# Batch 0's last stage in a new order of row tiles, and its FFN1 in two token passes

## The chip, the cores and the metric

The kernel runs on one core of a Trainium2 chip. The metric is device time in microseconds (us): the median of several executions. Profiles show one execution, in microseconds from the start of its span. TensorE is PE in them (PEld are its weight loads), VectorE is DVE, ScalarE is ACT, GpSimd is POOL, and SyncE is SP.

## The reference

Eight batches of 448 tokens. An attention of 12 heads of 64 channels without softmax is followed by a Fourier mix over tokens and channels, a layer norm, and a two-layer network, each added to the stream:

```
scores = q @ k.T / sqrt(64);  attn = max(scores, 0)**2 / 448;  x = attn @ v      # (8, 448, 768)
mixed = real(fft(fft(x, axis=tokens), axis=channels));  u = x + mixed
un = (u - mean(u)) / sqrt(var(u) + 1e-6)                                          # over the 768 channels
out = u + max(un @ w_ch1, 0) @ w_ch2                                              # 768 -> 3072 -> 768
```

## The kernel before

The Fourier mix of the tokens is symmetric: the kernel computes 225 of the 448 rows (0 to 224) as a "top" and gets the others as a "bottom" in reversed order. It therefore keeps u in two DRAM tiles per batch, `utop` (tokens 0 to 223) and `ubot` (tokens 224 on), and writes the bottom with an indirect DMA on POOL whose row indices run backwards (`back`). The add at the end (`reload`, `add`) reads u again from both.

The order of all instructions is fixed when the program is built. Each part is a generator that yields what its next step needs (`need(engine, duration, ...)`), and a small planner (`Streams.run`) always takes the step that can start earliest by its own cost estimates. Each engine then executes its list in order. Waits between engines are semaphores that the tile framework adds from what each instruction reads and writes. That holds for DRAM tiles too: two writes of one tile are ordered.

PSUM has three double-bank tiles (`BS`, `psS`) and two single banks (`BF`, `psF`). Attention's scores (L537), squares (L558, L564) and values (L522) of batch b+1 run among the FFN matmuls of batch b. FFN1 (L1073) computes the hidden rows for a group of tokens, 24 blocks of 128 rows with six matmuls each; a relu (L1044 on DVE, L1046 on ACT) writes each block to `hT`; FFN2 (L1091) then runs over tiles of 128 tokens. The groups alternate between 384 and 512 tokens, so that two batches make seven tiles: group 0 holds tokens 0 to 383 of batch 0, and group 1 the last 64 of batch 0 and all of batch 1.

Batch 0 has nothing to overlap with and has a stage of its own, `first_tail`. It takes four row tiles: `t` = 0 and 2 are the top (128 and 112 rows), 1 and 3 the bottom (128 and 112 rows), some of them computed twice. For each of them

- `rows` (L605, L609) makes u in PSUM, in two halves of 384 channels,
- `stats`, `aggregate`, `root` and `scale` give mean and 1/std,
- `copy` (L658) brings u to SBUF for the store, and `norm` gives `un`: on POOL from the SBUF copy for tiles 0, 1 and 2 (L682), on ACT and DVE from PSUM for tile 3 (L684, L687),
- `turn` (L708) transposes `un` on PE, and `unload` (L723) copies it to `unT`, the moving operand of FFN1. Two turns are preceded by filler matmuls (L706) and one is followed by 16 of them (L713). A fifth turn (L775) brings the last 64 tokens into group 1.

`first_stores` issues the four stores of u: tiles 0 and 2 on SP (L876), tiles 1 and 3 on POOL (L879). The loads that POOL issues in the same stretch come from `load_group` (L300, q, k and v) and from `load_w2` (L339, four pieces of 1152 KB of the second weight matrix; here w2_0 to w2_3). FFN1 of group 0 starts when all four tiles are in `unT`.

Of the kernel before, what the change touches and what calls it, by code (L numbers as in the profile page):

```python
# [117 lines left out]
def mm(n):  # L118
    return n / 2400 + 0.006
# [18 lines left out]
def kernel(  # L138
# [54 lines left out]
    back = [const.tile([128, 1], mybir.dt.int32, name=f"back{i}") for i in range(2)]  # L193
    warm = const.tile([128, 512], BF16, name="warm")
# [386 lines left out]
    def first_tail(pcs):  # L581


        pus, helds, done, sts = [None] * 4, [None] * 4, [[None, None] for _ in range(4)], [None] * 4
        mvs, stds, rss, nms, uts, pts = ([None] * 4 for _ in range(6))
        t_st, t_mv, t_std, t_rn = ([0.0] * 4 for _ in range(4))
        t_un, t_u = [[0.0, 0.0] for _ in range(4)], [[0.0, 0.0] for _ in range(4)]

        def rows(t):
            ch, i = divmod(t, 2)  # L590
            s0, s1 = SC[ch]
            n = s1 - s0
            d = 4 * mm(D // 2) + 3 * 0.06
            e = yield need("PE", 2 * d, [pcs[0][1], pcs[1][1]] + x_ready[0], [BF, BF] if t == 3 else [BS])
            if t == 3:
                pu = helds[t] = [BF.take() for _ in range(2)]
            else:
                helds[t] = [BS.take()]
                pu = [helds[t][0][:, 0], helds[t][0][:, 1]]
            for hf in range(2):  # L600

                for w in range(2):
                    for a, (n0, n1) in enumerate(TC):
                        mat = seq[:n1 - n0, w, a, s0:s1] if w == 0 or i ^ hf else nseq[:n1 - n0, a, s0:s1]
                        nc.tensor.matmul(pu[hf][:n, 0:D // 2], lhsT=mat,  # L605
                                         rhs=pcs[a][0][:n1 - n0, w, hf:hf + D // 2],
                                         start=(w == 0 and a == 0), stop=False)
                for a in range(3):
                    nc.tensor.matmul(pu[hf][:n, a * 128:(a + 1) * 128],  # L609
                                     lhsT=xTc[5 - a if hf else a][:, i * XH + s0:i * XH + s1],  # L610
                                     rhs=rev if hf else ident, start=False, stop=(a == 2))
                done[t][hf] = e - (1 - hf) * d + LATENCY["PE"]
            pus[t] = [p[:n] for p in pu]
            if t == 3:
# [5 lines left out]
        def half(t, hf):  # L620

            return pus[t][hf][:, D // 2 - 1::-1] if hf else pus[t][hf][:, 0:D // 2]

        def stats(t, hf):
            n = SC[t // 2][1] - SC[t // 2][0]
# [3 lines left out]
            nc.vector.bn_stats(sts[t][:n, hf, :], pus[t][hf][:, 0:D // 2])  # L629

        def aggregate(t):
            n = SC[t // 2][1] - SC[t // 2][0]
            t_mv[t] = yield need("DVE", 0.2)
            mvs[t] = work.tile([128, 2, 2], FP32, name="mv", tag="mv", bufs=4)[:n]
            nc.vector.bn_aggr(mvs[t][:, 0, :], sts[t][:n])

        def root(t):
            n = SC[t // 2][1] - SC[t // 2][0]
            t_std[t] = yield need("ACT", 0.25, [t_mv[t] + LATENCY["DVE"]])
            stds[t] = work.tile([128, 2], FP32, name="std", tag="std", bufs=4)[:n]  # L640
            nc.scalar.activation(stds[t][:, 0:1], mvs[t][:, 0, 1:2], AF.Sqrt, bias=eps_t[:n])

        def scale(t):
            n = SC[t // 2][1] - SC[t // 2][0]
            e = yield need("DVE", 0.3, [t_std[t] + LATENCY["ACT"]])
            t_rn[t] = e + LATENCY["DVE"]
            rss[t] = work.tile([128, 2], FP32, name="rstd", tag="rstd", bufs=4)[:n, 0:1]
            nms[t] = work.tile([128, 2], FP32, name="nmr", tag="nmr", bufs=4)[:n, 0:1]
# [3 lines left out]
        def copy(t, hf, en):  # L652
            ch, i = divmod(t, 2)
            n = SC[ch][1] - SC[ch][0]
            e = yield need(en, (act if en == "ACT" else dve)(D // 2), [done[t][hf]], [BU[i]] if hf == 0 else [])
            if hf == 0:
                uts[t] = work.tile([128, D], FP32, name="u", tag=f"u{i}" if i else "u", bufs=2)
            (nc.scalar.copy if en == "ACT" else nc.vector.tensor_copy)(  # L658
                uts[t][:n, hf * (D // 2):(hf + 1) * (D // 2)], half(t, hf))
            t_u[t][hf] = e  # L660
            if t == 3:
                BF.give(helds[t][hf], e)
            if hf == 1:
                if t != 3:
                    BS.give(helds[t][0], max(t_u[t]))
                e = max(t_u[t])
                first_us[ch][i] = uts[t], e + LATENCY["ACT"], e
                u_done[ch][i].t = e + LATENCY["ACT"]

        def norm(t, hf, en):  # L670
            ch, i = divmod(t, 2)
            n = SC[ch][1] - SC[ch][0]
            deps = [t_rn[t]]
            if en == "POOL":
                deps.append(u_done[ch][i])
            d = {"ACT": act(D // 2), "DVE": dve(D // 2), "POOL": 2.0}[en]
            e = yield need(en, d, deps, [BUN[ch]] if i == 0 and hf == 0 else [])
            if uns[0][t] is None:
                uns[0][t] = work.tile([128, D], BF16, name="un", tag=f"un{t}", bufs=1)
            un = uns[0][t][:n]  # L680
            if en == "POOL":
                nc.gpsimd.tensor_scalar(un, uts[t][:n], rss[t], nms[t], op0=ALU.mult, op1=ALU.add)  # L682
            elif en == "ACT":
                nc.scalar.activation(un[:, hf * (D // 2):(hf + 1) * (D // 2)], half(t, hf), AF.Identity,  # L684
                                     bias=nms[t], scale=rss[t])
            else:
                nc.vector.tensor_scalar(un[:, hf * (D // 2):(hf + 1) * (D // 2)], half(t, hf), rss[t], nms[t],  # L687
                                        op0=ALU.mult, op1=ALU.add)
            t_un[t][hf] = e + LATENCY[en]
            if min(t_un[t]) or en == "POOL":  # L690
                half_un[ch][i].t = max(t_un[t])

        def turned_cols(t):

            return ((128, ident, 0, 128), (128, rev[:, 0:63], HS + 97, 63),
                    (96, ident[:96, :96], 128, 96), (97, rev[:97, 31:128], HS, 97))[t]

        def turn(t, k):
            n, idn, c0, w = turned_cols(t)
            un = uns[0][t]  # L700
            e = yield need("PE", 6 * 0.06 + 0.11 * k, [max(t_un[t])], [BS])
            pts[t] = [BS.take()]
            bank = [pts[t][0][:, 0], pts[t][0][:, 1]]
            for i in range(k):

                nc.tensor.matmul(bank[0][:, 0:256], lhsT=warm[:, 0:128], rhs=warm[:, 0:256], start=True, stop=True)  # L706
            for m in range(MC):
                nc.tensor.matmul(bank[m // 3][:, m % 3 * 128:m % 3 * 128 + w], lhsT=un[:n, m * 128:(m + 1) * 128],  # L708
                                 rhs=idn, start=True, stop=True)
            done[t] = [e + LATENCY["PE"]] * 2  # L710
            for i in range(16 if t == 1 else 0):

                nc.tensor.matmul(bank[0][:, 384:512], lhsT=warm[:, 0:128], rhs=warm[:, 0:128], start=True, stop=True)  # L713
            if t == 1:
                yield need("PE", 16 * 0.055)

        def unload(t, en):
            n, idn, c0, w = turned_cols(t)
            g = groups[0][2]
            src = pts[t][0][:, :, 0:384].rearrange("p h (m w) -> p h m w", w=128)[:, :, :, 0:w]  # L720
            dst = g[:, :, c0:c0 + w].rearrange("p (h m) w -> p h m w", h=2)
            last = yield need(en, (act if en == "ACT" else dve)(6 * w), [done[t][0]])
            (nc.scalar.copy if en == "ACT" else nc.vector.tensor_copy)(dst, src)  # L723
            BS.give(pts[t][0], last)
            first_un[t].t = last + LATENCY["ACT"]
# [437 lines left out]
```

## Time and profile before

| | |
|---|---|
| median of 3 runs (lowest to highest) | 609.27 us (608.72 to 610.45) |
| profiled execution: span, first to last instruction | 607.4 us |
| the same execution's time outside the span | not shown; median less span is 1.9 us |
| PE busy in the span | 595.4 us (98%) |
| first row matmul of `first_tail` (L605) | starts at 41.06 us |
| first FFN1 matmul of group 0 (L1073) | starts at 53.74 us |
| first FFN2 matmul of group 0 (L1091) | starts at 89.80 us |
| PE idle from 41.06 to 89.80 us | 0.91 + 0.35 + 0.51 us |

The span is that of one execution, and its steps are read from the trace; the median comes from other executions of the same program. A line of a timeline gives the start, the length, the engine, the source line, the operation with what it writes and reads, how often it comes, and the idle time before it with what ended that. The length of a run of matmuls includes the pipeline of the last one, so the spacing of matmuls is taken from start to start.

### The profile page before, as it was taken

What the parts mean: (1) busy time and instruction counts of PE and PEld (TensorE: products, weight loads), DVE (VectorE), ACT (ScalarE), POOL (GpSimd) and SP (SyncE); (2) the same over time, 40 slices, a digit from 0 to 9 for tenths busy, and PEclk for the clock granted to TensorE, in tenths of its full rate; (3) what the DMA queues carried; (4) which work ended last, traced back from release to release, by engine and by line L of the source; (5) the groups of instructions that cost most, each with busy time, mean ns of one, the idle gap of its engine ahead of it and who ended that gap; (6) DMA issues with size and microseconds to landing.
All of it is one profiled execution on the core that took longest, in us unless ns stands there. A gap on an engine that the chain in (4) does not pass through costs nothing.

```text
span 607.4 us, 10224 instructions
## 1 busy us (share of the span) xinstructions
PE 595.4 (98%) x4035; PEld 329.5 (54%) x4054; DVE 339.4 (56%) x766; ACT 293.3 (48%) x445; POOL 155.2 (26%) x200
## 2 busy tenths in 40 slices
PE   8999999989999999999999999999999999999997
PEld 7566556534555565555445565555445566654464
DVE  6977785876596568455834369645843447110011
ACT  5967661677544357436653167435761345014300
POOL 8433203311163137111710117210620006100000
PEclk9999999999999999999999999999999999999999
DMA  9999997888659967977593796985451215420022
GB/s 127 207 209 228 216 194 132 186 128 120 111 148 212 157 121 215 141 135 120 172 154 96 127 127 173 160 164 97 145 136 60 87 51 165 121 91 20 1 79 79
DMA packets 125216, 82.22 MB, mean 135 GB/s; under 512 B 76272, under 2 KB 113168, under 8 KB 125168
## 3 DMA queue, kind: packets, MB, share of 16 engines
q0 software_dynamic: 40320, 34.07, 34.4%
q1 hardware_dynamic: 84848, 47.50, 33.6%
q8 instruction: 32, 0.52, 0.4%
q14 instruction: 16, 0.13, 0.1%
HBM read 62.91 MB, written 26.69 MB: 148 GB/s over the span
## 4 chain that ended last, share of the span: by engine, by line
PE 83%; DVE 11%; ACT 4%; issue 1%; DVEq 0%; ACTq 0%
PE psF L1091 33%; PE psF L1073 32%; PE psF L522 6%; PE psS L537 6%; DVE sq L564 2%; PE psS L961 2%; ACT sq L558 2%; DVE stats L837 2%; PE psS L1113 1%; PE psS L805 1%; DVE u L826 1%; DVE u L825 1%; PE psS L605 1%; PE psF L421 1%; DVE tm L816 1%
## 5 line engine op out<-in xcount | busy, mean ns | idle before, releaser
L1073 PE MATMUL psF<-unT,w 128*128 128x384 bf16 (+1 forms) x1134 | 227.2, 352 | 1.4 <-issue 0.2
L558 ACT ACTIVATE sq<-psS 112x896 bf16<-112x896 f32 x192 | 164.8, 916 | 130.5 <-PE psS L537 130.4
L1091 PE MATMUL psF<-w,hT 128*128 128x384 bf16 (+2 forms) x1343 | 225.0, 326 | 0.8 <-DVE xT L448 0.7
L1091 PEld LDWEIGHTS <-hT 128*128 128x128 bf16 x1344 | 129.2, 98 | 93.4 <-issue 8.8
L1073 PEld LDWEIGHTS <-w 128*128 128x128 bf16 x1152 | 109.6, 98 | 109.3 <-issue 12.3
L1046 ACT ACTIVATE hT<-psF 128x512 bf16<-128x512 f32 (+1 forms) x180 | 98.6, 548 | 110.2 <-PE psF L1073 109.6
L564 DVE TENSOR_TENSOR sq<-sq 112x896 bf16<-112x896 bf16 x192 | 117.8, 635 | 44.6 <-ACT sq L558 43.3
L1054 DVE TENSOR_TENSOR o<-psF,o 128x384 f32<-128x384 f32 (+2 forms) x56 | 31.0, 553 | 106.2 <-PE psF L1091 105.9
L300 POOL DMA_DIRECT2D vn<-in_v_dram x24 | 17.3, 719 | 177.4 <-PE psF L522 156.9
L445 DVE TENSOR_SCALAR xT<-psF 128x224 bf16<-128x224 f32 x48 | 18.7, 389 | 71.7 <-PE psF L522 71.7
L537 PE MATMUL psS<-qkT 64*112 64x448 bf16 x384 | 52.3, 366 | 2.0 <-DVE unT L780 0.8
L522 PE MATMUL psF<-sq,vn 112*64 112x448 bf16 x384 | 45.9, 359 | 1.7 <-DVE sq L564 1.2
L825 POOL TENSOR_TENSOR u<-tp,xn 128x385 f32<-128x385 f32 (+1 forms) x14 | 15.5, 1108 | 117.0 <-DVE tp L816 94.7
L537 PEld LDWEIGHTS <-qkT 64*112 64x112 bf16 x384 | 20.8, 125 | 27.6 <-issue 21.6
L522 PEld LDWEIGHTS <-vn 112*64 112x64 bf16 x384 | 17.9, 109 | 24.2 <-issue 16.0
L854 POOL TENSOR_SCALAR un<-u,rstd,nmr 128x768 bf16<-128x768 f32 (+1 forms) x24 | 26.9, 1124 | 6.4 <-DVE nmr L846 6.0
L837 DVE BATCH_NORM_STATS2 stats<-u 128x6 f32<-128x384 f32 (+1 forms) x56 | 28.2, 539 | 0.0
L879 POOL DMA_INDIRECT ubot<-u,back x16 | 17.1, 1072 | 23.7 <-DVE hT L1044 19.3
L300 POOL DMA_DIRECT2D qn<-in_q_dram x21 | 15.3, 726 | 19.7 <-DVE qkr L389 10.8
L1113 PE MATMUL psS<-warm 128*128 128x126 bf16 (+1 forms) x204 | 17.9, 242 | 1.3 <-DVE warm L215 1.3
L448 DVE TENSOR_SCALAR xT<-psF 128x224 bf16<-128x224 f32 x48 | 18.4, 384 | 0.0
L456 DVE TENSOR_TENSOR fold<-xT 128x225 bf16<-128x225 bf16 x48 | 15.9, 331 | 2.1
(117 smaller groups left out, 369.1 us busy)
## 6 DMA issues: line engine op xcount, KB each, us to landing
out_dram<-o SPq DMA_DIRECT2D x27, 384.0 KB, 2.7
vn<-in_v_dram POOLq DMA_DIRECT2D x24, 224.0 KB, 5.0
qn<-in_q_dram POOLq DMA_DIRECT2D x21, 224.0 KB, 6.3
kn<-in_k_dram POOLq DMA_DIRECT2D x21, 224.0 KB, 7.2
w<-in_moe_w_ch_dram POOLq DMA_DIRECT2D x12, 384.0 KB, 14.1
w<-in_moe_w_ch_dram POOLq DMA_DIRECT2D x4, 1152.0 KB, 22.7
utop<-u SPq DMA_DIRECT2D x8, 384.0 KB, 2.6
o<-utop SPq DMA_DIRECT2D x8, 384.0 KB, 4.5
```

What stands on the lines that cost most here:

```text
L300: nc.gpsimd.dma_start(out=t, in_=src[b, hs].rearrange("h (p j) d -> p h (j d)", j=4))
L522: nc.tensor.matmul(av[h * Dh:(h + 1) * Dh, 0:S], lhsT=vn[:, c, h0 + h, :], rhs=sq[:, h, :], start=(c == 0), stop=(c == 3))
L537: nc.tensor.matmul(sc[:R, h, 0:S].rearrange("k (c q) -> k c q", c=4), lhsT=kT[ps, m % 2, c, :], rhs=qT[ps, m % 2], start=True, stop=True)
L558: nc.scalar.activation(r, sc[:R, :, 0:S], AF.Relu)
L564: nc.vector.tensor_tensor(r, r, r, op=ALU.mult)
L837: nc.vector.bn_stats(stats[:n, hf, :], u[:n, hf * (D // 2):(hf + 1) * (D // 2)])
L854: nc.gpsimd.tensor_scalar(un[:n], u[:n], rstd[:n, i:i + 1], nmr[:n, i:i + 1], op0=ALU.mult, op1=ALU.add)
L1046: nc.scalar.activation(h[:, 0:N], ph[:, 0:N], AF.Relu)
L1054: nc.vector.tensor_tensor(o[:, hs], pc[:, 0:w], o[:, hs], op=ALU.add)
L1073: nc.tensor.matmul(ph[:, 0:N], lhsT=w1_sb[m][hf][:, jj * 128:(jj + 1) * 128], rhs=unT[:, m, 0:N], start=(m == 0), stop=(m == MC - 1))
L1091: nc.tensor.matmul(pc[:, 0:w], lhsT=hT[j][:, c * 128:(c + 1) * 128], rhs=w2_sb[j // 6][:, j % 6, hs], start=(j == 0), stop=(j == JC - 1))
L1113: nc.tensor.matmul(first_pps[0][:, t, c0:512], lhsT=warm[:, 0:128], rhs=warm[:, c0:512], start=not begun, stop=False)
```

## The change

The four row tiles of batch 0 become 128, 128, 96 and 96 tokens and hold each token once: tile 0 is the top's rows 0 to 127, tile 1 the bottom's 128 rows that mirror 1 to 128, tiles 2 and 3 the rest. Group 0 now takes its tokens in this order (its third tile holds tile 2 and the first 32 columns of tile 3), group 1 the last 64 columns of tile 3 and batch 1. Reloads and output stores follow the token order in pieces.

`first_tail` runs `rows` of tiles 0, 1 and 2 one after the other, then tiles 0 and 1 to the end: their norms on ACT and DVE from PSUM, their turns into the two `psF` banks, their unloads split over ACT and DVE. Tile 3's `rows` stand among these steps. The rest of tiles 2 and 3 (`copies`, `later`) becomes streams of their own, which the planner places among the FFN's work: their norms run on POOL from the SBUF copies. The filler matmuls and the fifth turn are gone. Each tile's store is placed by itself (`store`).

FFN1 of group 0 runs in two passes over the 24 blocks: one on columns 0 to 255 (tiles 0 and 1), two blocks in a `psF` bank, and one on columns 256 to 383, four blocks in a bank; the second waits for all four tiles. The first needs tiles 0 and 1 alone. `hT` becomes six tiles of four blocks. Other groups run as before.

In the built program POOL's order from the w2 loads on was: w2_0, v, w2_1, w2_2, norm of tile 0, norm of tile 1, norm of tile 2, store of tile 1, w2_3, store of tile 3, loads of q, k and v. It is now: w2_0, v, w2_1, w2_2, w2_3, store of tile 1, norm of tile 2, store of tile 3, norm of tile 3, loads of q, k and v. On PE the six matmuls of tile 2's turn stand behind 18 of FFN1's first-pass matmuls, those of tile 3's turn behind 36.

```diff
+    first_back = [const.tile([128, 1], mybir.dt.int32, name=f"fback{i}") for i in range(2)]
...
+        for i, x in enumerate(first_back):
+            nc.gpsimd.iota(x, pattern=[[0, 1]], base=HS - 1 - 128 * i, channel_multiplier=-1)
...
+        widths = (128, 128, R - 16, R - 16)
...
+        def copy(t, hf):
+            i = t % 2
+            e = yield need("ACT", act(D // 2), [done[t][hf]], [BU[i]] if hf == 0 else [])
...
+            nc.scalar.copy(uts[t][:widths[t], hf * (D // 2):(hf + 1) * (D // 2)], half(t, hf))
+            t_u[t][hf] = e
+            if hf == 1:
+                copied[t].t = e + LATENCY["ACT"]
+                sch.add(store(t), (1, 1))
...
+        def store(t):
+            ch, i = divmod(t, 2)
+            n = widths[t]
+            if i:
+                e = yield need("POOL", 1.1, [copied[t]])
+                nc.gpsimd.indirect_dma_start(
+                    out=ubot[0], out_offset=bass.IndirectOffsetOnAxis(ap=first_back[ch][:n], axis=0),
+                    in_=uts[t][:n], in_offset=None)
+            else:
+                e = yield need("SP", 0.1, [copied[t]])
+                nc.sync.dma_start(out=utop[0][ch * 128:ch * 128 + n], in_=uts[t][:n])
+            u_stored[0][t].t = sch.dma(e, n * D * 4) + i
...
+        def norm(t, hf):
...
+            if hf is None:
+                e = yield need("POOL", 1.1, [t_rn[t], copied[t]])
+                nc.gpsimd.tensor_scalar(uns[t], uts[t][:widths[t]], rss[t], nms[t], op0=ALU.mult, op1=ALU.add)
+                t_un[t] = [e + LATENCY["POOL"]] * 2
+                used[t].t = e
+                return
+            en = ("ACT", "DVE")[hf]
...
+        def turn(t):
+            n = widths[t]
+            e = yield need("PE", 6 * 0.06, [max(t_un[t])], [BF, BF] if t < 2 else [BS])
...
+        def unload(t, hf):
+            n = widths[t]
+            en, cp = (("ACT", nc.scalar.copy), ("DVE", nc.vector.tensor_copy))[hf]
+            e = yield need(en, (act, dve)[hf](3 * n), [t_turn[t]])
...
+            for g, c0, w0, w1 in ((0, t * 128, 0, n),) if t < 3 else ((0, 352, 0, 32), (1, 0, 32, 96)):
+                cp(groups[g][2][:, 3 * hf:3 * hf + 3, c0:c0 + w1 - w0], src[:, :, w0:w1])
...
+        def later(t):
+            for hf in range(2):
+                yield from stats(t, hf)
+            yield from aggregate(t)
+            yield from root(t)
+            yield from scale(t)
+            yield need("SP", 0.0, [copied[t]])
+            free(t)
+            yield from norm(t, None)
+            yield from turn(t)
+            e = yield from unload(t, 0)
+            yield from unload(t, 1)
...
         for t in range(3):
-            yield from rows(t)
-            if t == 2:
-                yield from rows(3)
-            yield from stats(t, 0)
...
-        yield from copy(3, 1, "DVE")
+            for hf in range(2):
+                yield from rows(t, hf)
+        for step, t, *hf in ((stats, 0, 0), (copy, 0, 0), (stats, 0, 1), (aggregate, 0), (copy, 0, 1), (root, 0),
+                             (stats, 1, 0), (copy, 1, 0), (scale, 0), (norm, 0, 0), (stats, 1, 1), (aggregate, 1),
+                             (norm, 0, 1), (root, 1)):
+            yield from step(t, *hf)
+        free(0)
+        for step, t, *hf in ((turn, 0), (scale, 1), (norm, 1, 0), (norm, 1, 1), (rows, 3, 0), (unload, 0, 1), (unload, 0, 0),
+                             (turn, 1), (rows, 3, 1), (unload, 1, 0), (unload, 1, 1), (copy, 1, 1)):
+            yield from step(t, *hf)
+        free(1)
         tail[0] = 2
-        sch.add(turn_rows(uns[0][1], max(t_un[1]), 128, rev[:, 63:127], 0, 64, "DVE", second_un[0]), (1, 1))
+        for t in (2, 3):
+            sch.add(copies(t), (0.05 * t, 0.05 * t))
+            sch.add(later(t), (0.05 * t, 0.05 * t))
...
-            for t0, n in ((0, 384), (384, 512)):
+            for segs, n in (([(0, 128), (HS + 96, 128), (128, 128)], 384), ([(256, 64), (S, S)], 512)):
...
+        def first(k, c0, w):
+
+            for j0 in range(0, JC, k):
+                hf = j0 // (JC // 2)
+                for i in range(k):
+                    j = j0 + i
+                    q = j // 4
+                    e = yield need("PE", 6 * mm(w), [w1_ready[hf]] + (first_un if c0 else []),
+                                   ([] if i else [BF]) + ([BH[q]] if hT[q] is None else []))
...
+                    for m in range(MC):
+                        nc.tensor.matmul(ph[:, i * w:(i + 1) * w], lhsT=w1_sb[m][hf][:, jj * 128:(jj + 1) * 128],
+                                         rhs=unT[:, m, c0:c0 + w], start=(m == 0), stop=(m == MC - 1))
...
+                sch.add(relu(ph, e, j0, k, c0, w), (0, 0))
+            return e
+
+        if b == 0:
+            yield from first(2, 0, 256)
+            e = yield from first(4, 256, 128)
+        else:
+            e = yield from first(1, 0, N)
```

More of the change, by code (lines that the diff above doesn't have):

```diff
@@ L581, in first_tail @@
     def first_tail(pcs):
[L584 to L589, printed above, removed]
-            ch, i = divmod(t, 2)
[L591 to L614, printed above, removed]
@@ new lines, in half, with rows @@
+        def half(t, hf):
+            return pus[t][hf][:, D // 2 - 1::-1] if hf else pus[t][hf][:, 0:D // 2]
+        def rows(t, hf):
+            i, n = t % 2, widths[t]
+            e = yield need("PE", 4 * mm(D // 2) + 3 * 0.06, [pcs[0][1], pcs[1][1]] + x_ready[0], [] if hf else [BS])
+            if hf == 0:
+                held[t] = BS.take()
+                pus[t] = [held[t][:n, h] for h in range(2)]
+            pu = pus[t][hf]
+            for w in range(2):
+                for a, (n0, n1) in enumerate(TC):
+                    mat = seq[:n1 - n0, w, a, span(t, 0)] if w == 0 or i ^ hf else nseq[:n1 - n0, a, span(t, 0)]
+                    nc.tensor.matmul(pu[:, 0:D // 2], lhsT=mat, rhs=pcs[a][0][:n1 - n0, w, hf:hf + D // 2],
+                                     start=(w == 0 and a == 0), stop=False)
+            for a in range(3):
+                nc.tensor.matmul(pu[:, a * 128:(a + 1) * 128], lhsT=xTc[5 - a if hf else a][:, span(t, i * XH)],
+                                 rhs=rev if hf else ident, start=False, stop=(a == 2))
+            done[t][hf] = e + LATENCY["PE"]
+            if t == 3 and hf == 1:
@@ L670, in norm @@
[L670 to L715, printed above, removed]
@@ new lines, in free @@
+        def free(t):
+            BS.give(held[t], max([t_st[t]] + t_u[t] + ([x - 0.15 for x in t_un[t]] if t < 2 else [])))
+        def turn(t):
+            n = widths[t]
+            e = yield need("PE", 6 * 0.06, [max(t_un[t])], [BF, BF] if t < 2 else [BS])
+            pts[t] = [BF.take(), BF.take()] if t < 2 else [BS.take()]
+            bank = pts[t] if t < 2 else [pts[t][0][:, h] for h in range(2)]
+            for m in range(MC):
+                nc.tensor.matmul(bank[m // 3][:, m % 3 * 128:m % 3 * 128 + n], lhsT=uns[t][:, m * 128:(m + 1) * 128],
+                                 rhs=rev[:n, 128 - n:] if t % 2 else ident[:n, :n], start=True, stop=True)
+            pts[t].append(bank)
+            t_turn[t] = e + LATENCY["PE"]
@@ L1001, in mixes @@
             yield from mix(b)
[L1004 removed]
+    BH = [Bufs(1) for _ in range(JC // 4)]
     BO = Bufs(2)
@@ L1013, in ffn, with pieces @@
     def ffn(b):
-        T0, N, unT = groups[b]
+        segs, N, unT = groups[b]
         NC = N // 128
+        tokens = [t for t0, n in segs for t in range(t0, t0 + n)]
+        def pieces(c, bounds=False):
+            out, r = [], 0
+            while r < 128:
+                t, w = tokens[c * 128 + r], 1
+                while r + w < 128 and tokens[c * 128 + r + w] == t + w and not (bounds and (t + w) % HS == 0):
+                    w += 1
+                out.append((r, t, w))
+                r += w
+            return out
         work_us = JC * MC * mm(N) + NC * 2 * JC * mm(D // 2)
         os, ot = [None] * NC, [Cell() for _ in range(NC)]
-        hT, ht = [None] * JC, [Cell() for _ in range(JC)]
+        hT, ht = [None] * (JC // 4), [Cell() for _ in range(JC)]
         def advance(us):
```

183 lines of the change are left out of this document (74 added, 109 removed).

## The prediction

> **What bounds the kernel now.** I read the page first, then TensorE's timeline over batch 0's tail, then GpSimd's timeline and waits, then the landing times of single DMAs.
>
> ```profile
> PE 595.4 (98%) x4035; PEld 329.5 (54%) x4054; DVE 339.4 (56%) x766; ACT 293.3 (48%) x445; POOL 155.2 (26%) x200
> DMA  9999997888659967977593796985451215420022
> ```
>
> TensorE (PE) is busy 98% of the span and executes in order, so a change is worth the PE work it removes plus the PE idle it removes, less what it adds of either. The second line says the DMA engines are full over the first 15% of the span, where this change lies (0 to 91 us).
>
> TensorE's timeline at the end of the tail and at the first FFN2 matmul (columns: start, us, engine, line, op, count, idle before):
>
> ```profile
> 50.27 0.42 PE L708 MATMUL psS<-ident,un 96*128 96x96 bf16 x6
> 51.60 0.44 PE L708 MATMUL psS<-rev,un 97*128 97x97 bf16 x6 [0.91 <-ACT un L684]
> ...
> 52.90 0.40 PE L537 MATMUL psS<-qkT 64*112 64x448 bf16 x2 [0.35 <-DVE unT L723]
> ...
> 53.74 1.15 PE L1073 MATMUL psF<-unT,w 128*128 128x384 bf16 x6
> ...
> 65.73 0.95 PE L522 MATMUL psF<-sq,vn 112*64 112x448 bf16 x8 [0.51 <-ACT hT L1046]
> ...
> 89.80 2.11 PE L1091 MATMUL psF<-w,hT 128*128 128x384 bf16 x12
> ```
>
> From the first row matmul (41.06) to FFN2 (89.80) PE idles only 0.91+0.35+0.51 = 1.77 us. That, some filler matmuls and one turn are all there is to win.
>
> GpSimd's (POOL) timeline, then its longest waits on the stores:
>
> ```profile
> 49.16 0.98 POOL L682 TENSOR_SCALAR un<-u,rstd,nmr 112x768 bf16<-112x768 f32 x1 [0.64 <-DVE nmr L650]
> 50.31 1.11 POOL L879 DMA_INDIRECT ubot<-u,back  x1 [0.17 <-issue]
> 51.44 0.88 POOL L339 DMA_DIRECT2D w<-in_moe_w_ch_dram  x1
> 71.62 1.01 POOL L879 DMA_INDIRECT ubot<-u,back  x1 [19.30 <-DVE hT L1044]
> 72.62 0.75 POOL L300 DMA_DIRECT2D qn<-in_q_dram  x1
> ```
> ```profile
> POOL ubot L879 <- DVE hT L1044: 19.3, 1, 19.3
> ```
>
> This is the row that decides. The second indirect store into ubot0 stands 19.3 us. The releaser named is an unrelated relu; what ends the wait is the landing of the first store, which writes the same DRAM tile. First the landing of the store issued at 50.31, then of the w2 pieces issued at 43.49, 44.62 and 51.44:
>
> ```profile
> DMA to landing us min/median/max: 20.4/20.4/20.4
> ```
> ```profile
> DMA to landing us min/median/max: 20.2/20.2/20.2
> ```
> ```profile
> DMA to landing us min/median/max: 25.1/25.1/25.1
> ```
> ```profile
> DMA to landing us min/median/max: 26.9/26.9/26.9
> ```
>
> So w2_1 lands at 63.7, w2_2 at 69.7, the store at 70.7, w2_3 at 78.3: POOL's transfers land in the order of issue, each 1152 KB piece taking 5.5 to 7.6 us. And POOL is held as a whole: the load behind the second store started at 72.62, right after it. Before, nothing that PE needs soon stood behind that store; all three norms on POOL were ahead of it.
>
> **The change, part by part.**
>
> *Removed on PE.* Filler 5+3 matmuls of 256 columns (0.55+0.33 us at a spacing of 0.11) and 16 of 128 (0.89 at 0.0555), and the fifth turn (64 columns, 0.27): 2.04 us. With the 1.77 of idle, 3.81 us at best.
>
> *FFN1 of group 0.* 144 matmuls of 384 columns at 4.00/24 = 0.167 us (24.0) become 144 of 256 at 0.110 (L706's spacing) and 144 of 128 at 0.0555 (L713's spacing): 23.8. Zero. The merged relus are fewer (18 for 24) and beside PE.
>
> *The tail's new order.* Two engines' reads of one PSUM tile are kept in order, as ScalarE's timeline of before shows:
>
> ```profile
> 44.37 0.48 ACT L658 COPY u<-psS 128x384 f32<-128x384 f32 x1 [1.30 <-DVE stats L629]
> ```
>
> The copy only reads what the stats read, and waits for them. So stats and copies of a half alternate between VectorE (0.56) and ScalarE (0.48), about 0.1 per hand-over. Walking this with those durations: norm of tile 0 half 0 on ScalarE (0.68) ends at 46.9, half 1 on VectorE at 47.8; tile 1's at 48.9 and 49.6; its unloads end near 51.1. PE waits about 0.5, 0.7, 0.5 and 0.7 around the two turns, starts FFN1 at 52.1, then waits some 2.1 for ScalarE, whose first relu stands behind the four copies of tiles 2 and 3, and 0.6 around the next unload: 5.1 of new idle for 1.77 taken out. PE reaches the turn of tile 3 at about 60.4.
>
> *Tile 3's norm moves to POOL, behind the stores.* In the built program's order POOL has: w2_2, w2_3, store of tile 1, norm of tile 2, store of tile 3, norm of tile 3. The store of tile 3 waits for the landing of the store of tile 1 (both write ubot0), and norm 3 is queued behind it. PE's six turn matmuls of tile 3 wait for norm 3, and they stand inside FFN1's first pass, ahead of 108 of its 144 matmuls: all of PE waits. Also, w2_3 is now issued ahead of the store of tile 1 (at 45.5, when the q load issued at 39.13 has landed 6.4 us later), so the store lands behind one more 1152 KB piece. Landing: w2_1 at 63.7 as before; w2_2 and w2_3 at 5.5 each (w2_1's time; the transposes L477 that slowed them before, from 63.2, now wait for PE) 74.7; the store 1.0 later, as before: 75.7. With w2_3 at its old 7.6 and w2_2 at 69.7 it is 78.3, and 75.0 if the pieces take 5.15. Then 0.9 to the next issue (70.7 to 71.62 before), 1.0 for it, 0.1, and 0.98 for the norm (L682), 0.2 to PE: the turn starts at 78.9. PE stands still from 60.4 to 78.9, 18.5 us. Nothing covers this; ScalarE and VectorE run out of work too.
>
> *After the turn.* What remains on PE up to FFN2, counted in the built order and priced by spacings of the timeline and the chain: the turn (0.35), 108 FFN1 matmuls of 256 (11.9) and 144 of 128 (8.0), five groups of value matmuls L522 at 0.88 (4.4), six groups of score matmuls L537 at 0.71 and a pair at 0.33 (4.6), 32 transposes L421 (1.0): 30.25. The relus and squares beside it had 18 us to catch up, so I add no wait.
>
> *A cold array.* At the run's start PE's matmuls came 0.105 us apart until about 7.1, and the same 126 columns 0.055 afterwards, though the clock column says 1.00 there:
>
> ```profile
> 1.27 5.44 PE L1113 MATMUL psS<-warm 128*128 128x512 bf16 x44 [1.27 <-DVE warm L215]
> 9.93 0.72 PE L1113 MATMUL psS<-warm 128*128 128x126 bf16 x10
> ```
>
> If 18.5 us of standing still brings that state back, 5.8 us at half speed lose 2.9; if not, 0. No idle this long is in the trace; I take 2.9, the nearest row, and keep both ends. The Trainium skill, "TensorE: Matmul & The Clock Gate", Part 1, says that an idle window of about 3.4 us halves the clock and a busy one of 3.4 restores it; by that the loss is 1.7 (an estimate) and the sum 1.2 lower.
>
> *The rest at nothing.* Two more iotas on POOL fall into its 8.8 us of idle before 39.13. Reloads and output stores change in pieces, not bytes; the first reload from ubot0 needs store 3, landed by about 82, and its add comes after 109. POOL's next loads start at 79 instead of 72.6, but their readers on PE are 22 us later. If these covers failed, the loads would cost up to the 7 us by which they are late; PE's own delay rules it out.
>
> *Sum.* 78.9 + 30.25 + 2.9 = 112.05 for FFN2's start, against 89.80: +22.25. After it the work and the waits (2.2 us around 122 to 126) are the same. The span is 607.4 and the median of the runs 609.27; I leave the 1.9 us around the span as they are: **631.5**.
>
> **The rivals.**
>
> *A. The store of tile 1 lands early.* If it took the 7.3 us of the second store before, it would land at 58.2 and norm 3 be ready for PE at 61.4, hardly after its 60.4. Then the time is -3.8 + 5.1 + 1.0 (61.4 against 60.4) = +2.3: 611.6; landing before 57 it is +1.3: 610.6. Against it: 20.4 us for just this store. The Trainium skill, "DMA: Bandwidth & Descriptors", Anatomy of one DMA, gives about 2 us plus the bytes at 436 GB/s, under 3 us here (an estimate); the 20.4 measured decides against it. Chance 0.04.
>
> *B. Faster.* As A, and the tail's hand-overs cost less than I walked: PE's new idle falls below 3.8. With 2 us of it, 607.5; 605.5 with none. It decides at the turn of tile 3: norm 3 must be done by about 58. For it: filler and waits do go. Against it: POOL's 19.3 us row. Chance 0.04.
>
> *C. The narrow pass is bound by weight loads.* LDWEIGHTS takes 98 ns a piece (L1073), longer than a 128-column matmul's 55. If loads did not overlap, 144 x 0.0425 = 6.1 us more, on top of the hold: 637.6. Against it: L713, 16 matmuls each with its 98 ns load, 0.0555 apart. The Trainium skill, "TensorE: Matmul & The Clock Gate", Back-to-back issue gap, gives about 81 ns sustained at 128 columns: +3.7, 635.2 (an estimate). Chance 0.06.
>
> **How the numbers follow.** The hold as summed has 0.86, C 0.06, A 0.04 (its two prices stand on either side of 0.3%, so half of it counts as no change), B 0.04. The low end takes a warm array (-2.9), the landing at 75.0 (-0.7) and a microsecond of the later waits gone: 627. The high end takes the landing at 78.3 (+2.6) and two waits after the standstill that I did not walk, of the size of those near 122 and 125 (0.83 and 1.04): 636. A measurement of this kernel can tell about 0.3% (1.8 us) from no change: faster 0.04 (B), same 0.02, slower 0.94.
>
> **What would show it.** In the profile after: PE idle of about 18 us before six matmuls psS<-rev,un 96x96, near 60 to 79, put down to POOL un; POOL's second DMA_INDIRECT near 76.6 with 20 us or more of idle before it; the first one landing some 25 us after its issue near 51; matmuls after the wait about twice as far apart for some microseconds; first FFN2 matmul at about 112. The prediction is wrong if the first store lands before 60, if norm 3 starts ahead of the second store, or if PE's turn of tile 3 shows no long idle.

## The result, and the profile after

The changed kernel takes 629.91 us in the median (629.49 to 631.12), against 609.27 for the kernel before beside it: the ratio is 1.034 (95% interval 1.032 to 1.036), slower by 3.4%. The prediction was 631.5 with a range of 627 to 636. The profiled execution took 629.49 us with a span of 627.7.

From the page of the kernel after, the busy times, TensorE's row and the row of its granted clock:

```profile
PE 596.0 (95%) x4149; PEld 336.6 (54%) x4168; DVE 336.8 (54%) x765; ACT 295.0 (47%) x447; POOL 155.3 (25%) x201
PE   8996099999999999999999999999999999999997
PEclk9999589999999999999999999999999999999999
```

TensorE is as busy as before (596.0 us for 595.4) in a span that is 20.3 us longer. One slice of 15.7 us is empty, and the granted clock is down in the same slice and the next.

TensorE's timeline of the kernel after (start, us, engine, line, op, count, idle before), at the places shown of before:

```profile
54.96 0.39 PE L424 MATMUL psF<-ident,qn 112*64 112x112 bf16 x8 [1.63 <-ACT hT L1044]
...
57.87 1.48 PE L1082 MATMUL psF<-unT,w 128*128 128x256 bf16 x12
78.66 0.66 PE L710 MATMUL psS<-rev,un 96*128 96x96 bf16 x6 [19.31 <-POOL un L687]
79.12 4.03 PE L1082 MATMUL psF<-unT,w 128*128 128x256 bf16 x24
...
91.74 2.79 PE L1082 MATMUL psF<-unT,w 128*128 128x256 bf16 x24
94.47 0.78 PE L540 MATMUL psS<-qkT 64*112 64x448 bf16 x6
...
99.56 2.85 PE L1082 MATMUL psF<-unT,w 128*128 128x128 bf16 x48
102.36 0.95 PE L525 MATMUL psF<-sq,vn 112*64 112x448 bf16 x8
...
111.54 3.09 PE L1107 MATMUL psF<-w,hT 128*128 128x384 bf16 x18
```

The idle of 19.31 us stands at the turn of tile 3, from 59.35 (57.87 + 1.48) to 78.66, and is put down to POOL's norm. This idle is called the hold below. The 24 products behind it take 4.03 us; the same 24 take 2.79 at 91.74. FFN2 starts at 111.54 instead of 89.80, 21.74 later.

GpSimd's timeline of the kernel after, and the landing times of its two indirect stores:

```profile
50.30 1.09 POOL L672 DMA_INDIRECT ubot<-u,fback  x1 [3.31 <-ACT u L657]
...
76.60 0.98 POOL L672 DMA_INDIRECT ubot<-u,fback  x1 [21.28 <-issue]
77.62 0.98 POOL L687 TENSOR_SCALAR un<-u,rstd,nmr 96x768 bf16<-96x768 f32 x1
```
```profile
DMA to landing us min/median/max: 3.3/14.4/25.5
```

The store of tile 1 is issued at 50.30 and lands 25.5 us later, at 75.8; the second store is issued at 76.60 and lands after 3.3. Norm 3 follows its issue at once. Before, the same wait was nearly as long (19.30 us, now 21.28), with only loads behind it. One queue order has turned a wait that cost nothing into one that stops TensorE.

### The profile page after: what moved, and what is told of

It is laid out like the page before. It is cut to its first block, busy times and chain, and to the rows that moved or that the text cites. A ratio compares the mean times of both kernels' runs of the same rounds, so it can differ in the third digit from the quotient of the medians.

```text
span 627.7 us, 10433 instructions
## 1 busy us (share of the span) xinstructions
PE 596.0 (95%) x4149; PEld 336.6 (54%) x4168; DVE 336.8 (54%) x765; ACT 295.0 (47%) x447; POOL 155.3 (25%) x201
## 4 chain that ended last, share of the span: by engine, by line
PE 79%; DMA 7%; issue 5%; DVE 5%; POOL 2%; ACT 2%; DVEq 0%; POOLq 0%; SPq 0%; ACTq 0%
PE psF L1082 32%; PE psF L1107 32%; PE psF L525 5%; PE psS L540 5%; PE psS L951 2%; DMA w<-in_moe_w_ch_dram 2%; DMA qkT<-qkr 2%; DMA qn<-in_q_dram 1%; PE psS L795 1%; DMA vn<-in_v_dram 1%; DVE stats L827 1%; DMA ubot<-u,fback 1%; DVE u L816 1%; ACT sq L561 1%; POOL qk L303 1%
## 5 line engine op out<-in xcount | busy, mean ns | idle before, releaser
L1082 PE MATMUL psF<-unT,w 128*128 128x512 bf16 (+3 forms) x1278 | 229.8, 333 | 2.3 <-DVE xT L451 0.8
L1082 PEld LDWEIGHTS <-w 128*128 128x128 bf16 x1296 | 118.3, 98 | 105.2 <-issue 13.6
L567 DVE TENSOR_TENSOR sq<-sq 112x896 bf16<-112x896 bf16 x192 | 119.5, 639 | 41.2 <-ACT sq L561 39.7
L815 POOL TENSOR_TENSOR u<-tp,xn 128x385 f32<-128x385 f32 (+1 forms) x14 | 17.4, 1240 | 117.2 <-DVE tp L806 105.6
L540 PEld LDWEIGHTS <-qkT 64*112 64x112 bf16 x384 | 20.8, 125 | 25.9 <-issue 20.3
L827 DVE BATCH_NORM_STATS2 stats<-u 128x6 f32<-128x384 f32 (+1 forms) x56 | 28.3, 541 | 0.0
L710 PE MATMUL psS<-rev,un 96*128 96x96 bf16 x6 | 0.7, 278 | 19.3 <-POOL un L687 19.3
L451 DVE TENSOR_SCALAR xT<-psF 128x224 bf16<-128x224 f32 x48 | 18.5, 385 | 0.0
L869 POOL DMA_INDIRECT ubot<-u,back x14 | 15.2, 1089 | 8.4 <-DMA ubot<-u,back 5.4
```

What stands on the lines that cost most here:

```text
L540: nc.tensor.matmul(sc[:R, h, 0:S].rearrange("k (c q) -> k c q", c=4), lhsT=kT[ps, m % 2, c, :], rhs=qT[ps, m % 2], start=True, stop=True)
L567: nc.vector.tensor_tensor(r, r, r, op=ALU.mult)
L827: nc.vector.bn_stats(stats[:n, hf, :], u[:n, hf * (D // 2):(hf + 1) * (D // 2)])
L1082: nc.tensor.matmul(ph[:, i * w:(i + 1) * w], lhsT=w1_sb[m][hf][:, jj * 128:(jj + 1) * 128], rhs=unT[:, m, c0:c0 + w], start=(m == 0), stop ...
```

## The experiments

My theory: norm 3 is late only because it stands on POOL behind a store that waits for the landing of another store into the same DRAM tile; landing is late because of the weight transfers ahead of it in POOL's queue; the long idle also lowers the clock. The rivals: the passes or the tail carry the loss, or the store's traffic itself does. Edits are to the changed kernel, where nothing else is said. The experiments ran beside runs of the kernel before that gave 609.40 us (first four kernels) and 610.51 us (last four); ratios are to those. The two differ because the granted clock of the kernel before falls for a while in some executions: with a mean clock of 1.00 (full) over the execution it took 609.07 and 609.24 us in the median (13 of 23 and 9 of 26 executions), with 0.993 to 0.997 it took 610.63 and 610.86. A ratio a few tenths of a per cent from 1 contains that.

### The second store into a DRAM tile of its own

```diff
+    ubot_low = dram.tile([UB, D], FP32, name="ubotlow")
-                    out=ubot[0], out_offset=...
+                    out=(ubot_low if ch else ubot[0]), out_offset=...
```

> Tile 3's reversed rows go to a DRAM tile of their own (the reload takes them from there), so that the second indirect store has nothing to wait for; the order of POOL's work stays store 1, norm 2, store 3, norm 3. Theory (POOL's sequence stands in the second store until the first one's bytes have landed, and norm 3 is behind it): the second store is issued right after norm 2, at about 55.4 us instead of 76.6, norm 3 ends at about 58 to 59, before TensorE arrives at the turn of tile 3 (59.35), and the 19.3 us of idle and the some 1.4 us of the slow array behind it go away: 629.9 - 20.7 = 609.2, and up to 1.4 us more if the later waits, which shrank in the changed kernel, grow back: 609 to 611. Rival, the passes and the tail walk: they stay as they are, so 628 to 630 if they carry the loss. Rival, the first store itself (it lands at 75.7 because three weight transfers are ahead of it in POOL's queue) holds something else than the second store's issue: time stays above 620 with the idle moved to another line.

Measured: 608.83 us, ratio 0.999 (0.997 to 1.000), just below the expected 609 to 611. GpSimd's timeline of this kernel, then TensorE's at the turn of tile 3, then the landing times of the two stores:

```profile
50.25 1.09 POOL L673 DMA_INDIRECT ubot<-u,fback  x1 [2.23 <-ACT u L658]
...
55.46 0.98 POOL L673 DMA_INDIRECT ubotlow<-u,fback  x1 [0.18 <-issue]
56.48 0.98 POOL L689 TENSOR_SCALAR un<-u,rstd,nmr 96x768 bf16<-96x768 f32 x1
```
```profile
59.40 0.42 PE L712 MATMUL psS<-rev,un 96*128 96x96 bf16 x6
```
```profile
DMA to landing us min/median/max: 23.9/26.1/28.3
```

The stores land 28.3 and 23.9 us after their issue, near 79, no earlier than in the changed kernel. Yet the 19.3 us are gone: the turn at 59.40 has no idle before it. It is neither the traffic nor the late landing that costs, but the write order of one DRAM tile, which makes POOL wait.

### Norm 3 ahead of the second store

```diff
-                e = yield need("POOL", 1.1, [copied[t]])
+                e = yield need("POOL", 1.1, [copied[t]] + ([used[t]] if t == 3 else []))
```

> Both stores go to the same DRAM tile as in the changed kernel, and the second still waits for the first; only the order on POOL differs: store 1, norm 2, norm 3, store 3. Theory (norm 3 is late only because it is behind the waiting store): norm 3 ends at about 57 to 58 us, TensorE does not stand at the turn of tile 3, 609 to 611 us; the second store's wait of some 20 us stays on POOL (it is issued at about 76.6 as before) and costs nothing, except that POOL's later query and value gathers behind it may come late: at most 1 to 2 us. Rival, that the stores' DRAM traffic or the store's late landing itself is what costs: 628 to 630, as the stores are issued and land as before. Rival, passes and tail: 628 to 630.

Measured: 608.80 us, ratio 0.9985 (0.9974 to 0.9997). In GpSimd's timeline of this kernel norm 3 starts at 55.41, and then comes the second store; TensorE's timeline follows:

```profile
79.28 0.98 POOL L672 DMA_INDIRECT ubot<-u,fback  x1 [22.89 <-DMA ubot<-u,fback]
```
```profile
56.83 0.42 PE L710 MATMUL psS<-rev,un 96*128 96x96 bf16 x6
...
90.94 3.09 PE L1107 MATMUL psF<-w,hT 128*128 128x384 bf16 x18
```

POOL still waits 22.89 us for the store, this time with the store named as what ended the wait, and TensorE does not notice. The loss of 21.1 us hangs on what stands behind the wait. The time fell slightly below the expected 609 to 611; in this trace TensorE waits for none of the loads behind the store. FFN2 starts at 90.94, though, against 89.80 in the kernel before: up to there the change still loses 1.1 us, and what it gains comes later.

### One weight transfer fewer ahead of the first store

```diff
-            e = yield need("POOL", 1.1)
+            e = yield need("POOL", 1.1, [stored_1] if i == 3 else [])
```

(`stored_1` is set when the store of tile 1 is issued; `i` counts the four pieces of w2.)

> The last of the four second-layer weight transfers on POOL's queue is issued behind the first indirect store instead of ahead of it; the order store 1, norm 2, store 3, norm 3 stays. Theory (the store's bytes land in the order of POOL's queue, behind the weights issued ahead of it, some 5 to 7 us for each such transfer): the store lands 5 to 7 us earlier (68.5 to 70.5 us), the second store's wait and TensorE's idle at the turn of tile 3 shrink by the same amount from 19.3 to 12 to 14 us, time 623 to 625. Rival (the landing is set by the total DMA traffic of the core at that time and not by the order within POOL's queue): the store lands at 74 to 76 as before, 628.5 to 630.5.

Measured: 625.23 us, ratio 1.025 (1.023 to 1.027), 4.7 us below the changed kernel. GpSimd's timeline, then TensorE's:

```profile
50.53 1.09 POOL L673 DMA_INDIRECT ubot<-u,fback  x1 [3.31 <-ACT u L658]
51.63 0.88 POOL L343 DMA_DIRECT2D w<-in_moe_w_ch_dram  x1
...
72.38 1.02 POOL L673 DMA_INDIRECT ubot<-u,fback  x1 [16.82 <-issue]
```
```profile
74.47 0.66 PE L713 MATMUL psS<-rev,un 96*128 96x96 bf16 x6 [14.88 <-POOL un L690]
```

The store landed 21.0 us after its issue, at 71.5 instead of 75.8, and the idle shrank from 19.31 to 14.88. That is less than I expected (landing at 68.5 to 70.5, idle of 12 to 14, 623 to 625 us): 4.3 us earlier and not 5 to 7. The landings of the single pieces show why. In the changed kernel w2_2 is issued at 45.10 and lands after 24.1 us, at 69.2; w2_3 is issued at 46.17 and lands after 28.7, at 74.9; the store lands 0.9 behind it. So w2_3 took 5.7 us. Here w2_2 is issued 1.3 us later, at 46.40, and lands after 24.2, at 70.6; the store again lands 0.9 behind. The piece is worth 5.7 us, and 1.4 of them were lost ahead of it, on transfers that the edit leaves in place. The order in POOL's queue does set what the store lands behind; when the pieces ahead are issued counts as well.

### Unused products in the hold: 165 and 192

```diff
+            for _ in range(165 if t == 3 else 0):
+                nc.tensor.matmul(bank[0][:, 0:256], lhsT=warm[:, 0:128], rhs=warm[:, 0:256], start=True, stop=True)
```

> The changed kernel with 165 unused 256-column products of a constant tile ahead of the turn of tile 3, into the bank that the turn then overwrites: 165 x 0.11 = 18.2 us of work in the 19.3 us in which TensorE stands. The hold itself stays. It measures what the slow array after the standstill costs. By the trace of the changed kernel (24 products of 3.96 us of spacing instead of 2.71, the turn 0.1 longer) about 1.4 us: 628.4 to 628.7, and the run of 24 behind the turn at 2.7 to 2.8 us. By the 2.9 us that the prediction took: 627.0. If the later waits take it back: 629.9, no change. If the products run longer than 0.11 each or the hold is shorter, they delay the turn and the time rises instead.

Measured: 629.51 us, ratio 1.031 (1.029 to 1.033); not told from the changed kernel. TensorE's timeline of this kernel, then windows of it (us, PE busy and instructions, granted clock, DMA share, GB/s):

```profile
79.65 0.43 PE L712 MATMUL psS<-rev,un 96*128 96x96 bf16 x6 [2.53 <-POOL un L687]
79.92 4.45 PE L1084 MATMUL psF<-unT,w 128*128 128x256 bf16 x24
```
```profile
80.00:81.00 1.00, 1.00 (x10) 0.72 0.08 31
...
82.00:83.00 1.00, 1.00 (x6) 0.50 1.44 194
```

In this execution the hold ended a microsecond later than in the changed kernel's profile, and 2.53 us of idle were left. That was enough: the clock fell to 0.50 at about 80.4, when TensorE had already been working again for 0.8 us, and the 24 products were slow all the same. The profiled execution did not remove what it was to remove. The other four have no trace, and they differ: 627.58 and 627.78 us at a mean clock of 0.999 and 1.00, inside the 627.0 to 628.7 expected without the slow products, but also 629.51 at 1.00 and 630.10 at 0.997. So I ran it with more products:

```diff
-            for _ in range(165 if t == 3 else 0):
+            for _ in range(192 if t == 3 else 0):
```

> The changed kernel with 192 unused 256-column products ahead of the turn of tile 3: 192 x 0.110 = 21.1 us, from 58.9 to about 80.0, past the end of the hold, which was at 78.6 to 79.6 in two profiles. TensorE then never stands and the turn comes 0.4 to 1.4 us later than it could. Theory (the granted clock falls to 0.50 because TensorE stood, and comes back only 3.0 to 4.5 us after it works again): the clock stays at 1.00 and the 24 products behind the turn take 2.8 us instead of the 4.0 to 4.7 of the three kernels with the hold; their time loss of 1.4 to 2.2 us goes and the lateness of the turn comes: 628.5 to 630. Rival (the products are slow because of the transfers released at the hold's end, which move 190 GB/s in the same microseconds): the 24 products take 4 us or more though the clock column shows 1.00, and the time is 630.5 to 631.5.

Measured: 629.74 us, ratio 1.032 (1.030 to 1.035). TensorE's timeline, and a window with the released transfers:

```profile
59.33 21.12 PE L710 MATMUL psS<-warm 128*128 128x256 bf16 x192
80.29 0.42 PE L712 MATMUL psS<-rev,un 96*128 96x96 bf16 x6
80.55 2.79 PE L1084 MATMUL psF<-unT,w 128*128 128x256 bf16 x24
...
111.73 3.09 PE L1109 MATMUL psF<-w,hT 128*128 128x384 bf16 x18
```
```profile
82.00:83.00 1.00, 1.00 (x12) 1.00 1.43 190
```

With the same 190 GB/s beside them the 24 products take 2.79 us: standing still slows them, not the transfers. From the turn to FFN2 it is 111.73 - 80.29 = 31.44 us, in the changed kernel 111.54 - 78.66 = 32.88: the lowered clock costs 1.44 us there. The total does not show it, because the unused products end after norm 3 (79.39) and delay the turn.

### FFN1 in one pass, without the hold

On the kernel with norm 3 ahead of the second store:

```diff
-            yield from first(2, 0, 256)
-            e = yield from first(4, 256, 128)
+            yield need("PE", 0.0, first_un)
+            e = yield from first(1, 0, N)
```

> The order store 1, norm 2, norm 3, store 3 on POOL (no hold), and the first group's FFN1 in one pass over all 384 tokens, which then waits for all four turns. It shows what the two passes are worth once nothing holds them. Theory: with the passes FFN1 starts at 51.3 us, and 3.1 us of its products and 2.0 us of idle lie between there and the unload of tile 3's turn (about 58.8); in one pass that stretch holds only attention work brought forward, so 2 to 3 us more of idle, against the 0.8 to 0.9 us of wider spacing that the passes cost: 610 to 611.5, or 1.2 to 2.5 us above the two-pass order (608.8). Rival, the attention work brought forward fills the stretch and the passes buy nothing: 608.0 to 608.3, faster by their wider spacing. Rival, the narrow passes are bound by weight loads as the prediction's third rival had it: faster by 3.7 to 6.1 us, 603 to 605.

Measured: 611.54 us, ratio 1.0023 (1.0008 to 1.0037), at the upper end of what was expected. Against the two passes with norm 3 ahead of the second store (608.80, ratio 0.9985) the one pass is 0.4% slower, 2.3 us by the ratios and 2.7 by the times; the passes pay once nothing holds them. That it is the idle, as I expected, is not shown, because the clock fell as well. TensorE's timeline of this kernel:

```profile
49.59 0.48 PE L710 MATMUL psF<-rev,un 128*128 128x128 bf16 x3 [0.48 <-DVE unT L721]
49.86 0.84 PE L616 MATMUL psS<-pc,seqm 128*96 128x384 bf16 x2
```

In the changed kernel the same two products take 0.49. Here the clock is at 0.50 from about 49.6 to 53.0 us and from 56.4 to 63.3, and the mean clock was 0.991 to 0.997 in all 12 executions, against 0.999 to 1.00 in all 12 with the two passes. TensorE was busy in most of these 10.3 us, so the clock alone could account for the whole difference. How it divides between idle and clock was not separated. The narrow-pass rival is refuted: without the passes nothing became faster.

### Two waits of the tail taken away

First, tile 3's second half ahead of the turn of tile 1 (on the kernel with norm 3 first):

```diff
-        ... (norm, 1, 1), (rows, 3, 0), (unload, 0, 1), (unload, 0, 0), (turn, 1), (rows, 3, 1), ...
+        ... (norm, 1, 1), (rows, 3, 0), (rows, 3, 1), (unload, 0, 1), (unload, 0, 0), (turn, 1), ...
```

> As the order store 1, norm 2, norm 3, store 3 (no hold, 608.8), and the second half of tile 3's row products moves ahead of the turn of tile 1, so that the 0.17 and 0.48 us in which TensorE waits for the banks of turn 0 are covered by 0.9 us of work. Theory: FFN1 starts 0.6 us earlier, at 50.7, and if nothing behind it gives that back the time is 608.2. Rival: the wait of 1.6 us behind ScalarE's first relu takes it up, since ScalarE's copies and VectorE's statistics of tiles 2 and 3 set that time: 608.6 to 608.9, the idle there 2.0 to 2.2 us.

Measured: 609.39 us, ratio 0.999 (0.997 to 1.000): no gain. As the rival said, TensorE's wait behind ScalarE's relu took it up (1.93 us for 1.63):

```profile
54.78 0.39 PE L424 MATMUL psF<-ident,qn 112*64 112x112 bf16 x8 [1.93 <-ACT hT L1044]
...
55.30 1.28 PE L1082 MATMUL psF<-unT,w 128*128 128x256 bf16 x6
```

And a lowered clock came on top: six products take 1.28 us here, 0.83 without it. Six of the 12 executions had a mean clock of 0.997 as this one (609.82 us in the median), the other six 1.00 (608.64, inside the rival's 608.6 to 608.9). Then, besides, the statistics and copies of tiles 2 and 3 in alternation:

```diff
-        for t in (2, 3):
-            sch.add(copies(t), (0.05 * t, 0.05 * t))
+        for hf in range(2):
+            for t in (2, 3):
+                yield from stats(t, hf)
+                yield from copy(t, hf)
+        for t in (2, 3):
             sch.add(later(t), (0.05 * t, 0.05 * t))
...
         def later(t):
-            for hf in range(2):
-                yield from stats(t, hf)
             yield from aggregate(t)
```

> As the kernel with tile 3's rows ahead of the turn of tile 1, and besides the statistics (VectorE) and copies (ScalarE) of tiles 2 and 3 alternate between the two tiles by halves instead of going through tile 2 and then tile 3, so that the one engine reads one tile while the other engine reads the other. Theory (ScalarE's first relu is late because copy and statistics of one tile's bank take turns, 4 x 1.1 us one behind the other): the last copy ends at about 52.9 instead of 54.2, the first relu follows at once, the 1.6 us wait of TensorE falls to 0.3 to 0.6 us, FFN2 starts at 89.0 to 89.6 instead of 90.9, time 606.8 to 607.6, faster than before by 0.3 to 0.4%. Rival: the norms of tiles 2 and 3, FFN1's second bank or the attention chain (ScalarE's squares) set the time a little later: 608.2 to 608.9.

Measured: 607.70 us, ratio 0.9955 (0.9940 to 0.9971), faster than both kernels and 0.1 us above the expected 606.8 to 607.6. ScalarE's timeline, then TensorE's:

```profile
50.91 2.10 ACT L657 COPY u<-psS 96x384 f32<-96x384 f32 x4 [0.50 <-DVE stats L632]
...
53.10 0.58 ACT L1045 ACTIVATE hT<-psF 128x512 bf16<-128x512 f32 x1
```
```profile
53.27 0.39 PE L424 MATMUL psF<-ident,qn 112*64 112x112 bf16 x8 [0.34 <-DVE qkT L429]
...
56.23 0.43 PE L710 MATMUL psS<-rev,un 96*128 96x96 bf16 x6 [0.70 <-POOL un L687]
...
89.82 3.09 PE L1108 MATMUL psF<-w,hT 128*128 128x384 bf16 x18
```

The four copies run without a pause, the relu starts 1.0 us earlier than with norm 3 first (53.10 for 54.08), and the wait behind it is gone. FFN2 starts at 89.82, 0.2 later than the expected range, because norm 3 on POOL is now last (0.70). In the kernel before it starts at 89.80.

## Why the prediction was right, by its steps

- **The hold.** Predicted: landing at 75.7, second store at 76.6, turn at 78.9. Measured: 75.8, 76.60, 78.66. The experiments confirm the cause from both sides: the write order alone taken away, and norm 3 alone moved, each bring the 21 us back.
- **The landing.** This was right step by step, not only in the sum: w2_2, w2_3 and the store were put at 69.2, 74.7 and 75.7 and landed at 69.2, 74.9 and 75.8. The price of one more transfer, 5.5 us, measured 5.7; moving that transfer gave 4.3, for the reason given there. With the second store in a tile of its own and with norm 3 first, the same piece took 7.0 and 7.3 us.
- **The walk of the tail.** The steps were right, the sizes too large. The four waits around the turns, in the timeline below, are 0.32, 0.47, 0.17 and 0.48 (taken as 0.5, 0.7, 0.5, 0.7), the wait behind the relu 1.63 (2.1), and the last one (0.6) is not there: 3.07 in place of 5.1. TensorE arrived at 59.35 instead of 60.4 and stood 19.31 instead of 18.5 us. Behind a landing that does not depend on it this error cost nothing, but the prices of the first two rivals rested on it.

```profile
46.64 0.34 PE L710 MATMUL psF<-ident,un 128*128 128x128 bf16 x3 [0.32 <-ACT un L695]
47.45 0.34 PE L710 MATMUL psF<-ident,un 128*128 128x128 bf16 x3 [0.47 <-DVE un L697]
...
48.78 0.33 PE L710 MATMUL psF<-rev,un 128*128 128x128 bf16 x3 [0.17 <-ACT unT L721]
49.59 0.33 PE L710 MATMUL psF<-rev,un 128*128 128x128 bf16 x3 [0.48 <-DVE unT L721]
49.76 0.49 PE L616 MATMUL psS<-pc,seqm 128*96 128x384 bf16 x2
```

- **FFN1's passes at nothing.** This term was too small. From start to start of the next line, the 24 products of 256 columns at 91.74 take 2.73 us (0.114 each, 0.110 taken), and 48 of 128 columns, from 99.56 to 102.36, take 2.80 (0.058, 0.0555 taken): 144 x (0.004 + 0.003) = about 1 us. The spacings came from repeated products on one constant tile; these have a new operand each time; that this makes the difference was not tried. Weight loads do not bound them: the third rival's 98 ns is far above the 58 measured. The Trainium skill gives about 81 ns sustained at 128 columns ("TensorE: Matmul & The Clock Gate", Back-to-back issue gap); the 58 measured here decide against it.
- **After the turn.** 30.25 us of work were predicted, 31.44 measured without the lowered clock: 0.8 from the wider spacing of the 252 products left, 0.27 from one wait behind a relu.
- **The cold array.** This step was mis-sized: 2.9 taken from the run's start, 1.44 measured. Reckoned in the same way, the hold with one transfer fewer and the one with 165 products lost 2.16 and 1.67. The run's start was the wrong row to compare with: there the clock column shows 1.00 beside slow products, here it shows 0.50. In the kernel after, the clock is at 1.00 again 3.0 us after TensorE resumed (about 81.7). The estimate of 1.7 by the Trainium skill ("TensorE: Matmul & The Clock Gate", Part 1), from a busy window of about 3.4 us, came closer; the way back took 3.0 us here, 4.2 and 4.5 in the two other kernels. Together with the work after the turn the step came out at 32.88 in place of 33.15: one term was too small, the other too large, and that the errors nearly cancel is luck.
- **Later waits taken as unchanged.** They were not. From FFN2's start to the end of the span it was 607.4 - 89.80 = 517.6 us before and is 627.7 - 111.54 = 516.2. Before, TensorE waited 0.83, 1.04 and 0.15 us around 122 to 125; after, 0.47 and 0.39 at the like place. That is 1.2 of the 1.4 us. With FFN2's start 0.5 earlier than predicted they make 1.9; the prediction was 1.6 too high, because the median lies 0.4 above the profiled execution. Which of the removed steps had caused these waits was not tried.
- **The rivals.** The store did not land early. The faster case and the early landing (610.6 to 611.6) show themselves in the kernels without the hold: 608.8, lower than both prices of the early landing, because new idle was 2 us less and the later waits shrank, while the wider spacing took about 1 us back.

## What to carry to other kernels

Before moving a step onto a queue, look up what stands ahead of it there and what that waits for: a wait that costs nothing today is paid by whatever is queued behind it tomorrow. Two stores into one DRAM tile are ordered even when their rows differ; a tile of its own, or one swap in the queue, was worth 21 us here. Without the hold the change measured 0.15% faster (0.03 to 0.26%); with row products moved into a wait, and two engines reading two tiles in alternation rather than the same tile in turns, it was 0.45% (0.29 to 0.60%). Read such small gains against the clock. Next to those executions of the kernel before that had a mean clock of 1.00 (609.07 and 609.24 us), the two kernels at 608.80 and 607.70 are 0.04% and 0.25% faster; their own clock was 0.999 to 1.00 in every execution. And FFN2 starts at 90.94 and 89.82 in them, at 89.80 before, so in these traces the stretch that was changed has not become shorter: what was gained lies behind it.

## What was not expected of the hardware

The granted clock reacts late, and to short idles. It fell to 0.50 between 2.3 and 5.3 us after TensorE's last product (the hold with one weight transfer fewer: 59.6 to 61.9; the kernel after: 59.35 to 64.6), and behind the holds it came back 3.0 to 4.5 us after TensorE resumed (4.5 in the hold with one transfer fewer, 74.5 to 78.9). An idle of 2.53 us was enough, and in the kernel with tile 3's rows first one of 1.93 us with shorter ones just before; there the clock was down from about 55.5 to 58.9:

```profile
56.00:57.00 1.00, 1.00 (x10) 0.50 1.11 315
```

The Trainium skill ("TensorE: Matmul & The Clock Gate", Part 1) asks for an idle window of about 3.4 us; where the shorter idles measured here lowered the clock too, the measurement decides.

The length of one idle does not settle it. In the one-pass kernel's trace the clock fell at about 49.6 us, behind waits of 0.33, 0.47, 0.17 and 0.48; in the changed kernel's it stayed at 1.00 behind the same waits and behind the 1.63 at 54.96. With tile 3's rows first, half of the executions show the fall and half do not. No run here shows the rule. So an idle of 2 us can cost another microsecond behind it, where no wait is to be seen: 609.82 us with the fall, 608.64 without. The products that take longer and the clock column show it. In an execution without a trace the mean clock does: one fall to 0.50 for 3.4 us makes 0.997 of a span of 607.
